# Queries and keys in a tile each, instead of two tiles of half the tokens each

## The chip, the cores and the metric

The kernel runs on one core of a Trainium2 chip. The metric is the device time of one execution in microseconds, as the median of several runs. Profiles are of one execution and show what each engine did: TensorE (PE, with its weight loads as PEld), VectorE (DVE), ScalarE (ACT), GpSimd (POOL), and SyncE (SP), which issues the transfers between the chip's main memory and its on-chip memory.

## The reference

A block of attention followed by a gated block, on 2048 tokens of width 640, in 32-bit floating point. What matters here is the attention: 32 heads of 20 columns, each token looking at itself and the 255 tokens before it.

```python
B, S, D = x.shape
H = 32; Dh = D // H; W = 256
qkv = (x @ wqkv).reshape(B, S, 3, H, Dh).transpose(2, 0, 3, 1, 4)
q, k, v = qkv[0], qkv[1], qkv[2]
scores = jnp.einsum("bhqd,bhkd->bhqk", q, k) * (Dh ** -0.5)
mask = (idx[:, None] - idx[None, :] >= 0) & (idx[:, None] - idx[None, :] < W)
scores = jnp.where(mask[None, None], scores, -1e9)
p = _softmax(scores, axis=-1)
o = jnp.einsum("bhqk,bhkd->bhqd", p, v)
return o.transpose(0, 2, 1, 3).reshape(B, S, D) @ wo
```

Around it: `h = x + A(layernorm(x))`, and then a gated block with a 2048 x 2048 product over the tokens, `h2 = h + B(layernorm(h))`.

## The kernel before

The program is written out in full, without loops on the chip, and the orders of the instructions of PE, DVE, ACT and SP are those of the source; those of POOL are set by a planner when the program is built. Waits between engines and transfers are put in by the framework, from what each instruction reads and writes.

**Stages.** Up to about 180 us the input is normalized and the value projection is made (`vgemm`); then the query and key projection (`qk_item`), whose last 16 items (`dense_tail`) lie beside the first maxima; from 243 to about 470 us the attention loop runs; after that come the output projection and the gated block.

**Queries and keys.** To keep the precision of 32 bits in 16-bit products, each query and key value is split into three bf16 parts (`split_qk`, L579 to L596), and the parts are written to `qk_d` in main memory (L595). From there four heads at a time, a *stack*, are loaded: 6 x 20 = 120 partitions hold six pairings of parts, so that one matmul over 120 rows gives the full product. There are 8 stacks and three places for them on the chip, used in turn: `slot0`, `slot1` and `xb` (the last is memory in which the input's normalized columns lay before). A place consists of two tiles of 16 KB a partition. Before the change, tile b of a place holds the tokens of half b (0 to 1023 or 1024 to 2047): first the queries of the four heads, then their keys. `qk_d` is laid out in the same way, by half, so one row of one part has the four heads' 1024 tokens next to each other.

`load_stack` (L298) issues 24 transfers on SP for each stack, 12 for half 0 and 12 for half 1, each of 20 rows and 160 KB. For the first use of a place it sets 32 rows of the keys to a constant with two clears on POOL (L304), one for each tile; the rows 120 to 122 of the keys that remain of it meet the rows 120 to 122 of the queries, which hold the negative row maxima in three parts, so that a product over 123 rows gives the score less the maximum. A stack is loaded during the 16 steps in which the stack two before it is scored: one transfer in even steps, two in odd ones.

**The loop** (L735 to L777) takes 128 steps, 16 for each stack; a step works on 128 tokens and four heads. In step s, for each head `hh`:

- `max_item` (L327) makes the products for the row maxima of the tokens 16 steps ahead: four strips of 32 queries, each against 288 keys (L341), side by side in the array's columns; DVE takes the maximum (L351). Where the 288 keys cross token 1024, the helper `tokens` (L314) gives two pieces, and each piece is a matmul with its own weight load. Stack 0's maxima are made before the loop, with one matmul of 128 queries and up to 384 keys (L345).
- `score_item` (L373) makes the scores: four strips of 32 keys, each against 288 queries (L394), again in two pieces where they cross token 1024; ACT takes the exponential (L397; in the last stack two heads at once, L399), and POOL clears what lies outside the window (L401, L404).
- `pv_item` (L407) multiplies the step before last with the values (L422); every second step a block of results is copied out (L438, L440) and stored (L441).

Every 8 steps `max_rows` (L354) turns the maxima, splits them into three parts, stores them to `m_d` (L366) and loads them into rows 120 to 122 of the queries of the half concerned (L368): the first half 8 steps before the stack is scored, the second as its scoring begins.

## Time and profile before

| | us |
|---|---|
| median of 3 runs (1126.02 to 1129.81) | 1126.63 |
| the profiled execution | 1125.76 |
| its span, first to last instruction | 1124.0 |
| from the loop's first exponential (242.94) to the last stack's first (448.77) | 205.83 |

The page of the profile gives each engine's busy time, the transfers and the chain of work that ended last. A table by stretch gives, for stretches of time, their length, then the busy time and number of instructions of each engine shown, the granted share of PE's clock, the share of the 16 transfer engines that was busy, and GB/s. In a timeline, the brackets at the end of a row give the idle time of that engine before the row and what ended it; "issue" says that the engine waited for nothing that the profile shows. In rows by source line, the three numbers after the colon are the least, median and greatest duration in nanoseconds. The names of tiles are shown without their numbers, so `slot` is either tile of slot0 or slot1, and `slot,slot` two of them.

### The profile page before, as it was taken

The numbers are of one execution on the slowest core, as the hardware profiler recorded it, in microseconds if no ns is written. First come the engines' busy times: TensorE is split into PE (matmuls) and PEld (weight loads), VectorE is DVE, ScalarE is ACT, GpSimd is POOL, SyncE is SP. The second block draws the span as 40 slices with busy tenths as digits, with TensorE's granted clock in tenths as the row PEclk, the third lists the DMA queues.
The fourth block names the chain that finished last, engine by engine and source line by source line (L and its number), as shares of the span: only waits on it lengthen the run. The fifth ranks groups of instructions, "written<-read, shape, count | busy, mean of one in ns | idle before, by whom it ended". The sixth has DMA issues, their size and how long they took to land.

```text
span 1124.0 us, 28713 instructions
## 1 busy us (share of the span) xinstructions
PE 1089.4 (97%) x11139; PEld 980.3 (87%) x11139; DVE 752.8 (67%) x2070; ACT 567.5 (50%) x1155; POOL 319.6 (28%) x447
## 2 busy tenths in 40 slices
PE   8999999989999999999999999999999999999998
PEld 8998887657877777699899999999999899999998
DVE  6643444779988999588877678655358974556542
ACT  4444443248988899735566567434347521222210
POOL 4324446766766666723200011000001000000000
PEclk9999999989999999999999999999999999999999
DMA  7834567545555555689554522242251563444321
GB/s 256 283 113 135 171 186 248 183 157 181 179 179 172 177 178 165 170 249 311 218 195 167 182 91 76 75 134 90 104 171 57 180 209 119 124 148 148 98 87 60
DMA packets 87672, 180.57 MB, mean 161 GB/s; under 512 B 11440, under 2 KB 45760, under 8 KB 83648
## 3 DMA queue, kind: packets, MB, share of 16 engines
q1 hardware_dynamic: 87536, 178.74, 49.8%
q8 instruction: 87, 1.43, 0.5%
q14 instruction: 49, 0.40, 0.1%
HBM read 120.82 MB, written 57.88 MB: 159 GB/s over the span
## 4 chain that ended last, share of the span: by engine, by line
PE 72%; DMA 8%; ACT 7%; DVE 6%; issue 3%; POOL 2%; SPq 1%; DVEq 0%; POOLq 0%; ACTq 0%
PE g L1136 22%; PE out_ps L1201 8%; ACT pt L397 5%; PE pv L422 4%; PE zb L1028 4%; PE qk L568 3%; PE qk L569 3%; PE qk L570 3%; PE bank L341 3%; PE bank L394 3%; PE zx L976 2%; PE zv L976 2%; PE zy L976 1%; PE wo_ps L101 1%; DMA o_d<-ot 1%
## 5 line engine op out<-in xcount | busy, mean ns | idle before, releaser
L397 ACT ACTIVATE pt<-bank 128x384 f32<-128x384 f32 (+1 forms) x452 | 180.1, 478 | 26.4 <-PE bank L394 16.2
L803 ACT ACTIVATE aw<-fx 128x512 fp32r<-128x512 f32 (+2 forms) x160 | 93.7, 596 | 173.5 <-PE g L1136 120.7
L1136 PE MATMUL g<-zl,aw 128*128 128x432 f32 x768 | 171.0, 358 | 0.0
L351 DVE CUSTOM_DVE_ANT_0 junk<-bank,strip 128x288 bf16<-128x288 f32 x392 | 156.7, 454 | 16.3 <-PE bank L341 13.8
L1136 PEld LDWEIGHTS g<-zl,aw 128*128 128x128 f32 x768 | 143.6, 188 | 5.9
L422 PE MATMUL pv<-pt,v_sb 128*32 128x192 f32 (+3 forms) x1984 | 129.6, 323 | 6.2 <-ACT ot L438 3.8
L1136 PE MATMUL g<-ze,aw 128*128 128x432 f32 x576 | 134.0, 360 | 0.3 <-DVE row L797 0.2
L797 DVE TENSOR_TENSOR aw<-fx,aw 128x512 fp32r<-128x512 f32 (+2 forms) x160 | 102.7, 647 | 37.1 <-ACT aw L803 35.8
L1136 PEld LDWEIGHTS g<-ze,aw 128*128 128x128 f32 x576 | 107.0, 188 | 6.7 <-ACT aw L803 1.2
L401 POOL TENSOR_SCALAR_AFFINE_SELECT pt<-pt 128x512 f32<-128x512 f32 x128 | 83.9, 656 | 62.7 <-ACT pt L397 60.2
L394 PE MATMUL bank<-slot 123*32 123x288 bf16 (+7 forms) x1296 | 94.4, 276 | 4.9 <-ACT pt L397 3.5
L1201 PE MATMUL out_ps<-wout,y_sp 128*128 128x320 f32 (+1 forms) x630 | 96.2, 309 | 0.4 <-ACT y_sp L140 0.4
L341 PE MATMUL bank<-slot 120*32 120x288 bf16 (+6 forms) x1280 | 92.2, 277 | 3.6 <-issue 1.6
L1028 PE MATMUL zb<-win,aw 128*128 128x432 f32 x480 | 95.4, 359 | 0.0
L1201 PEld LDWEIGHTS out_ps<-wout,y_sp 128*128 128x128 f32 (+1 forms) x630 | 94.1, 188 | 1.2 <-ACT y_sp L140 0.7
L87 POOL TENSOR_TENSOR mvz<-mvz,half 128x1 f32<-128x1 f32 x16 | 10.1, 633 | 298.8 <-DVE mvz L86 296.8
L1028 PEld LDWEIGHTS zb<-win,aw 128*128 128x128 f32 x480 | 89.9, 187 | 5.0 <-ACT row L803 0.3
L422 PEld LDWEIGHTS pv<-pt,v_sb 128*32 128x32 f32 x1984 | 59.9, 110 | 18.1 <-issue 9.9
L797 DVE TENSOR_TENSOR row<-g,row 128x432 f32<-128x432 f32 x80 | 48.2, 604 | 37.8 <-PE g L1136 36.9
L394 PEld LDWEIGHTS <-slot 123*32 123x32 bf16 x1728 | 58.5, 97 | 15.3 <-issue 6.0
L404 POOL TENSOR_SCALAR_AFFINE_SELECT pt<-pt 128x512 f32<-128x512 f32 x112 | 71.4, 637 | 0.0
L351 DVE CUSTOM_DVE_ANT_0 junk<-bank,mask 128x384 bf16<-128x384 f32 (+2 forms) x120 | 51.7, 447 | 21.1 <-PE bank L345 15.8
(196 smaller groups left out, 2247.1 us busy)
## 6 DMA issues: line engine op xcount, KB each, us to landing
slot<-qk_d SPq DMA_DIRECT2D x144, 160.0 KB
fx<-wsp_in SPq DMA_DIRECT2D x32, 512.0 KB
qk_d<-sg SPq DMA_DIRECT2D x40, 384.0 KB
fx<-hn_d SPq DMA_DIRECT2D x32, 320.0 KB
o_d<-ot SPq DMA_DIRECT2D x64, 128.0 KB
xb<-qk_d SPq DMA_DIRECT2D x48, 160.0 KB
z_d<-row SPq DMA_DIRECT2D x16, 432.0 KB
g_d<-row SPq DMA_DIRECT2D x16, 432.0 KB
```

The lines of the kernel that those rows point to most:

```text
L341: nc.tensor.matmul(ps[32 * j:32 * j + 32, o:o + w], one(st, 120, 0, hh, q0, 32), k, start=True, stop=True, tile_position=(0, 32 * j))
L351: nc.vector.tensor_tensor_reduce(out=junk[:, :n], in0=ps[:, :n], in1=keep, scale=1.0, scalar=NEG, op0=OP.add, op1=OP.max, accum_out=m_cols ...
L394: nc.tensor.matmul(ps[32 * i:32 * i + 32, b + o:b + o + w], one(st, 123, 1, hh, k0, 32), q, start=True, stop=True, tile_position=(0, 32 * i))
L397: nc.scalar.activation(pt[:, hh, :n], ps[:, :n], AF.Exp, scale=SCALE)
L401: nc.gpsimd.affine_select(out=pt[:, :, :P], in_=pt[:, :, :P], pattern=[[0, 4], [1, P]], base=0, channel_multiplier=-1, compare_op=OP.is_ge ...
L404: nc.gpsimd.affine_select(out=pt[:, :, 256:], in_=pt[:, :, 256:], pattern=[[0, 4], [-1, P]], base=-1, channel_multiplier=1, compare_op=OP. ...
L422: nc.tensor.matmul(ps[32 * hh:32 * hh + 32, a - 512 * c:b - 512 * c], v_sb[:, kb, v0:v0 + 32], pt[:, hh, a - kb * P:b - kb * P], start=fir ...
L797: (eng or nc.vector).tensor_tensor(out=out, in0=a, in1=b, op=op)
L803: nc.scalar.activation(out, a, AF.Copy)
L1028: nc.tensor.matmul(b[0][:, :HF], a[t][:, x, kk], win2[0][:, y, kk, h * HF:(h + 1) * HF], start=kk + x + y == 0, stop=kk == KD - 1 and x == 1)
L1136: nc.tensor.matmul(ps, w[m][:, x, k], zc[k][m][:, y], start=start and k + x + y == 0, stop=stop and k == 3 and x == 1, skip_group_check=True)
L1201: nc.tensor.matmul(ps[j][:, :HD], src[:w, a, k, :], e1["wout"][:w, b, k, j * HD:(j + 1) * HD], start=(k == 0 and a + b == 0), stop=(k == K ...
```

## The change

A place's two tiles now hold the queries (tile 0) and the keys (tile 1) of all 2048 tokens, in place of the two halves; `qk_d` loses its axis of halves, so that a row of one part and head has its 2048 tokens next to each other. `tokens` gives one access for any window, and `one` is gone: score and maximum matmuls that cross token 1024 are one matmul each. The loads keep their number and order (12 for the tokens below 1024, then 12 for the others), but each now takes, for each of its 20 rows, four separate runs of 1024 tokens. Both clears of a place go to the key tile, two heads each.

```diff
-    qk_d = dram.tile([2, 3, 2, 2 * DH, H // 2, S // 4], F32, name="qk_d")
+    qk_d = dram.tile([2, 3, 2 * DH, H // 2, S // 2], F32, name="qk_d")
...
-            slot_ap[i] = [h.bitcast(BF16).rearrange("p (a h t) -> p a h t", a=2, h=4) for h in halves]
-            slot_w[i] = [h.bitcast(F32).rearrange("p (a h t) -> p a h t", a=2, h=4) for h in halves]
+            slot_ap[i] = [h.bitcast(BF16).rearrange("p (h t) -> p h t", h=4) for h in halves]
+            slot_w[i] = [h.bitcast(F32).rearrange("p (h t) -> p h t", h=4) for h in halves]
...
-            st = slot_w[g % 3]
+            st, T = slot_w[g % 3], S // 4
             if g < 3:
-                for h in st:
-                    nc.gpsimd.memset(h[96:P, 1], ONES)
+                for i in range(2):
+                    nc.gpsimd.memset(st[1][96:P, 2 * i:2 * i + 2], ONES)
                     if g == 2:
                         yield
             for b in range(2):
                 for j, parts in enumerate(((0, 0), (0, 1), (0, 2), (1, 0), (1, 1), (2, 0))):
                     for a in range(2):
-                        src = qk_d[g // 4, parts[a], b, a * DH:(a + 1) * DH, g % 4 * 4:g % 4 * 4 + 4]
-                        nc.sync.dma_start(st[b][j:6 * DH:6, a], src)
+                        t = slice(b * T, (b + 1) * T)
+                        src = qk_d[g // 4, parts[a], a * DH:(a + 1) * DH, g % 4 * 4:g % 4 * 4 + 4, t]
+                        nc.sync.dma_start(st[a][j:6 * DH:6, :, t], src)
                         yield
 
         def tokens(st, rows, a, hh, t0, n):
-
-            o = 0
-            while o < n:
-                c, t = divmod(t0 + o, S // 2)
-                w = min(n - o, S // 2 - t)
-                yield o, w, st[c][:rows, a, hh, t:t + w]
-                o += w
-
-        def one(st, rows, a, hh, t0, n):
-            (_, _, x), = tokens(st, rows, a, hh, t0, n)
-            return x
+            return st[a][:rows, hh, t0:t0 + n]
...
-                    for o, w, k in tokens(st, 120, 1, hh, lo + skip * j, n):
-                        nc.tensor.matmul(ps[32 * j:32 * j + 32, o:o + w], one(st, 120, 0, hh, q0, 32), k,
-                                         start=True, stop=True, tile_position=(0, 32 * j))
+                    nc.tensor.matmul(ps[32 * j:32 * j + 32, :n], tokens(st, 120, 0, hh, q0, 32),
+                                     tokens(st, 120, 1, hh, lo + skip * j, n),
+                                     start=True, stop=True, tile_position=(0, 32 * j))
             else:
-                for o, w, k in tokens(st, 120, 1, hh, lo, n):
-                    nc.tensor.matmul(ps[:, o:o + w], one(st, 120, 0, hh, qb * P, P), k, start=True, stop=True)
+                nc.tensor.matmul(ps[:, :n], tokens(st, 120, 0, hh, qb * P, P), tokens(st, 120, 1, hh, lo, n),
+                                 start=True, stop=True)
...
-            nc.sync.dma_start(slot_w[g % 3][b][120:123, 0], rows.rearrange("a (h r) c -> a h (r c)", h=4))
+            t = slice(b * S // 4, (b + 1) * S // 4)
+            nc.sync.dma_start(slot_w[g % 3][0][120:123, :, t], rows.rearrange("a (h r) c -> a h (r c)", h=4))
...
-                for o, w, q in tokens(st, 123, 0, hh, kb * P + b, e - b):
-                    nc.tensor.matmul(ps[32 * i:32 * i + 32, b + o:b + o + w], one(st, 123, 1, hh, k0, 32), q,
-                                     start=True, stop=True, tile_position=(0, 32 * i))
+                nc.tensor.matmul(ps[32 * i:32 * i + 32, b:e], tokens(st, 123, 1, hh, k0, 32),
+                                 tokens(st, 123, 0, hh, kb * P + b, e - b),
+                                 start=True, stop=True, tile_position=(0, 32 * i))
...
-                T = S // 4
-                base = qk_d[m // 5, 0, c // 2, m % 5 * 8, 0, c % 2 * 256:c % 2 * 256 + 256]
+                T = S // 2
+                base = qk_d[m // 5, 0, m % 5 * 8, 0, c * 256:c * 256 + 256]
                 nc.sync.dma_start(bass.AP(tensor=base.tensor, offset=base.offset,
-                                          ap=[[T, P], [2 * 2 * DH * H // 2 * T, 3], [1, 256]]), sg.bitcast(F32))
+                                          ap=[[T, P], [2 * DH * H // 2 * T, 3], [1, 256]]), sg.bitcast(F32))
```

## The prediction

> **What bounds the kernel now.** First the profile's page: the span and the engines' sums.

> ```profile
> span 1124.0 us, 28713 instructions
> ...
> PE 1089.4 (97%) x11139; PEld 980.3 (87%) x11139; DVE 752.8 (67%) x2070; ACT 567.5 (50%) x1155; POOL 319.6 (28%) x447
> ```

> These are averages over stages; the change touches one, the attention loop from 243 to 449 us. So next comes the table by stretch for L397, the exponentials: each stretch is one stack of 16 steps with the same 64 of them (65 where an edge cuts one).

> ```profile
> 242.94:272.49 29.55, 25.66 (x64) 0.93 0.56 174
> 272.49:301.16 28.67, 25.64 (x64) 1.00 0.56 172
> 301.16:331.63 30.47, 25.33 (x64) 1.00 0.58 176
> 331.63:361.62 29.99, 25.51 (x65) 1.00 0.56 174
> 361.62:390.78 29.16, 25.36 (x64) 1.00 0.58 176
> 390.78:418.88 28.10, 25.43 (x64) 1.00 0.59 179
> 418.88:448.77 29.89, 25.46 (x65) 1.00 0.56 165
> ```

> The first numbers are the stretch and its length. ACT's exponentials fill 25.4 of 28.1 us in the fastest stack, and ACT has the ot copies beside them, so ACT sets the pace. Yet equal stacks differ by up to 2.4 us. Over 28.10 the others spend 1.45 + 0.57 + 2.37 + 1.89 + 1.06 + 1.79 = 9.1 us. The timeline shows where the largest parts lie.

> ```profile
> 317.11 0.31 PE L394 MATMUL bank<-xb 123*32 123x288 bf16 x4 [2.35 <-issue]
> ...
> 349.19 0.26 PE L341 MATMUL bank<-slot 120*32 120x224 bf16 x1 [1.62 <-issue]
> ...
> 380.17 0.30 PE L394 MATMUL bank<-slot 123*32 123x288 bf16 x3 [1.02 <-issue]
> ```

> PE stands still for 2.35, 1.62 and 1.02 us, together 4.99, and waits for nothing that the profile names ("issue"). It isn't caught up: the stack with 2.35 is the longest. Counting steps of 1.76 us (28.10 / 16) from the stack's start, the halts begin 7.7, 9.1 and 10.0 steps in: in or just behind steps 6 to 9, where windows cross token 1024 and PE has the most instructions. (The halt ends at a row's start and lasted its bracketed time; a row's start less that is 314.76, 347.57, 379.15.) I read them as a wait for PE's own program, from the page's DMA queues, the DMA view of two neighbouring stretches (309.6 to 314.1 us, and on to 315.6) and the table by stretch that ends at each halt.

> ```profile
> q8 instruction: 87, 1.43, 0.5%
> ```

> ```profile
> q1 hardware_dynamic: 280, 0.71, 60.2%
> ```

> ```profile
> q8 instruction: 1, 0.02, 5.8%
> ```

> ```profile
> 311.23:314.76 3.53, 3.53 (x140) 3.00 (x129) 3.53 (x19) 3.43 (x10) 2.62 (x5) 1.00 0.58 152
> 343.58:347.56 3.98, 3.93 (x138) 3.20 (x127) 3.86 (x19) 3.49 (x10) 2.90 (x6) 1.00 0.58 179
> 374.99:379.15 4.16, 4.08 (x138) 3.23 (x130) 3.92 (x19) 3.85 (x11) 3.24 (x7) 1.00 0.58 192
> ```

> **Fewer matmuls.** Rows by source line; a row with two tiles ("slot,slot") is the piece of a split item whose weights lie in the other half, one for each split.

> ```profile
> L394 PE MATMUL bank<-slot,slot x160: 177/224/270, 253.6 to 432.7; 123*32 123x128 bf16 x20, 123*32 123x96 bf16 x20, 123*32 123x32 bf16 x20, 123*32 123x64 bf16 x20
> L394 PE MATMUL bank<-xb,xb x64: 177/224/271, 311.3 to 403.7; 123*32 123x128 bf16 x8, 123*32 123x96 bf16 x8, 123*32 123x32 bf16 x8, 123*32 123x64 bf16 x8
> L394 PE MATMUL pair<-slot,slot x32: 177/224/270, 456.8 to 459.1; 123*32 123x128 bf16 x4, 123*32 123x96 bf16 x4, 123*32 123x64 bf16 x4, 123*32 123x32 bf16 x4
> L341 PE MATMUL bank<-slot,slot x160: 179/226/275, 256.7 to 436.3; 120*32 120x224 bf16 x20, 120*32 120x192 bf16 x20, 120*32 120x256 bf16 x20, 120*32 120x160 bf16 x20
> L341 PE MATMUL bank<-xb,xb x64: 176/228/275, 286.4 to 378.1; 120*32 120x256 bf16 x8, 120*32 120x224 bf16 x8, 120*32 120x192 bf16 x8, 120*32 120x160 bf16 x8
> L345 PE MATMUL bank<-slot,slot x8: 231/250/284, 211.6 to 218.0; 120*128 120x256 bf16 x4, 120*128 120x128 bf16 x4
> ```

> 256 + 224 + 8 = 488 matmuls go, with a weight load each: 976 of 22278 PE instructions, some 4 of 87 blocks. The columns streamed stay the same. Steps 6 and 7 of a stack (scores) and 8 and 9 (maxima) lose 16 pieces each. What a piece costs directly I read in the fastest stack, by four steps: 2 to 5, the split 6 to 9, 10 to 13.

> ```profile
> 394.09:401.26 7.17, 6.91 (x212) 5.88 (x208) 6.62 (x35) 6.83 (x18) 4.90 (x8) 1.00 0.61 175
> 401.26:408.68 7.42, 7.32 (x261) 6.38 (x257) 7.20 (x37) 6.84 (x17) 5.55 (x10) 1.00 0.62 196
> 408.68:415.76 7.08, 6.81 (x201) 6.13 (x196) 6.51 (x34) 6.74 (x17) 4.90 (x8) 1.00 0.49 154
> ```

> 7.42 against a mean of 7.13 is 0.29 us for 64 pieces, 4.6 ns each, so at most 7 x 0.29 = 2.0 us; at least nothing, as ACT is busy 6.8 us in each. I take **1.0**. The 8 in the dense stage and the 32 of the last stack lie beside ACT, POOL and other PE work: nothing.

> **The halts.** Split steps issue 518 records in 7.42 us, a block in 3.67; the others 817 in 14.25, a block in 4.47. A late block thus gains 0.8 us of cover: the three halts shrink by 0.8 each, 2.4 in all. The remaining 4.1 us of excess (9.1 - 4.99) are start-up in the first stack and waits under 1 us, some of them late blocks too; where the cover was the short one they vanish. I give them 1.8. Bounds: nothing if blocks come later by as much as PE slows, 8 if none comes late. I take **4.2**. What is late next is ACT, already the pace.

> [...]

> **The loads.** 24 loads a stack, in the same order on SP's queue; each changes from 20 runs of 8 KB to 80 of 2 KB, the same 160 KB, because a row's 1024-token half is no longer next to the next head's. The maximum's rows go from 3 runs to 12, and the stores at L595 keep their 384 of 1 KB at other strides. SP's issue times (least, median and most, in ns), by source line:

> ```profile
> L311 SPq DMA_DIRECT2D slot<-qk_d x144: 694/702/1885, 160.1 to 418.1; - x144
> L368 SPq DMA_DIRECT2D slot<-m_d x12: 265/272/380, 220.3 to 452.2; - x12
> L595 SPq DMA_DIRECT2D qk_d<-sg x40: 359/366/424, 92.9 to 242.9; - x40
> L160 SPq DMA_DIRECT2D m<-o_d x32: 302/434/1474, 457.7 to 527.2; - x32
> ```

> Upper end for the issue: by runs, (702 - 272) / 17 = 25 ns each, 80 give 2.2 us. Lower end: 160 runs take 434 ns at L160 and 384 take 366 at L595, so runs cost nothing. I take 0.75 us, near those rows. SP is then busy 24 x 0.75 + 8 x 0.37 (the o_d stores, priced as L595's) + 1.2 (the maximum's two stores and two loads) = 22 of 28.1 us a stack. Nobody waits for a load until the next stack's first maximum, nor for the maximum's rows until some 5 steps after their issue: **nothing**, while a load's issue stays under 1.0 us. The bytes are the same; should small runs move worse, q1's share of the engines, 60.2% in the stretch above, may grow by two thirds before they are full.

> **The constants.** Six clears of 32 rows on POOL keep their size, but both of a stack now go to the key tile. For the third that is the second half of xb, free only after the last projection item; before, one half was free early.

> ```profile
> L304 POOL MEMSET xb<- x2: 1800/1802/1804, 219.8 to 237.5; 32x2048 f32 x2
> ...
> 242.94 2.42 ACT L397 ACTIVATE pt<-bank 128x384 f32<-128x384 f32 x6 [4.17 <-POOL sg L592]
> ```

> One clear runs at 237.5, ahead of the POOL work for which the first exponential waits 4.17 us. If the other goes there too, the loop starts 1.8 us later. If it goes behind that work, only the third stack's key loads wait, and behind them on SP the first ot stores, for which there are six buffers. That work is ready while the first clear runs and stands earlier in the program, so I take **0**, bounds 0 and +1.8.

> **The sum.** 1.0 + 4.2 = 5.2 us. The profiled execution took 1125.76 (span 1124.0): 1120.6 by its own time. The median of the runs is 0.87 higher, 1126.63: **1121.4**.

> **Rivals.**
> (a) The blocks stay late: requests and transfers keep their distance and PE halts elsewhere. For: the last stretch, 29.89, has excess outside the crossing steps. Against: the three largest halts are all in them. Only the direct 1.0 is left: 1125.6. 0.20.

> [...]

> (b) The second clear delays the loop: 1121.4 + 1.8 = 1123.2. 0.06.
> (c) PE's issue sets the pace: each piece costs a matmul's turn, 7.17 us over 212, 34 ns, and 488 of them 16.6 us: 1110.0. The split steps' 4.6 ns a piece speak against it. With the upper ends of my own two terms, 2.0 and 8, it is 1116.6. Together 0.10.

> [...]

> (d) Slower: SP becomes the bound. At 1.4 us a load SP needs 24 x 1.4 + 4.2 = 37.8 us a stack against 28.1; six stacks are loaded in the loop, 58 us, 1184. It decides above 1.0 us a load. L595 speaks against it, the odd 702 of L311 for it. 0.07.
> (e) Slower: waits are set for whole tiles. Then score items wait for the second half's maximum rows in the query tile, which they don't read until step 6; the store alone takes 3.7 us to land, the load behind it some more, so about 5 us in each of seven stacks: 1156. Against it: ACT writes a part of aw while PE reads another. 0.05.

> ```profile
> 303.11 3.70 DMA m_d<-m
> ```

> ```profile
> 720.19 0.36 PE L1136 MATMUL g<-ze,aw 128*128 128x432 f32 x1
> 720.20 0.63 ACT L803 ACTIVATE aw<-fx 128x512 fp32r<-128x512 f32 x1 [3.85 <-PE g L1136]
> ```

> **Numbers.** The forecast has 0.52. About 0.3%, 3.4 us, is what a measurement of this kernel can tell from no change. Faster: forecast and (c), 0.62; within: (a) and (b), 0.26; slower: (d) and (e), 0.12. The range runs from (c)'s 1116.6 to 1127.5, (a) with the runs' scatter (1126.02 to 1129.81), and leaves out (d), (e) and (c)'s first price.

> **What would show it.** PE with 10651 matmuls and some 83 blocks on q8; no row with two tiles at L394 and L341; stacks of 28 to 28.5 us; no "issue" halt over 1 us in steps 6 to 9; L311 near 0.75 us; the first exponential's wait near 4.2 us. Wrong: halts of the old size at other steps (a), 6 us before the first exponential (b), L311 over 1 us (d), score items that wait for the slot's rows (e).

## The result: 7% slower, and the profile after

| | before | after |
|---|---|---|
| median of 6 runs each, us | 1129.42 (1126.02 to 1130.80) | 1210.16 (1207.22 to 1212.48) |
| ratio, with its 95% interval | 1 | 1.072 (1.070 to 1.075) |
| span of the profiled execution | 1124.0 | 1207.3 |
| first exponential of the loop | 242.94 | 254.56 |
| seven stacks, to the last stack's first exponential | 205.83 | 267.88 |
| from there to the end | 675.2 | 684.9 |

The forecast was 1121.4, so it missed by 89 us and by the sign. Of the 83.3 us between the two spans, 62.1 lie in the seven stacks of the loop, 11.6 ahead of it and 9.7 behind it. The first lines of the page, after:

```profile
span 1207.3 us, 27703 instructions
...
PE 1112.6 (92%) x10651; PEld 987.8 (82%) x10651; DVE 755.9 (63%) x2070; ACT 571.7 (47%) x1155; POOL 316.6 (26%) x447
```

PE has the 10651 matmuls that the prediction asked for, and q8 84 packets, and yet PE's share fell from 97% to 92%: it waits. Next comes the table by stretch, of the exponentials (L389 after), one stack of 16 steps a row.

```profile
254.56:291.29 36.73, 25.77 (x65) 0.92 0.50 153
291.29:331.08 39.79, 26.23 (x64) 0.89 0.43 131
331.08:371.52 40.44, 25.95 (x64) 0.84 0.43 129
...
450.66:488.75 38.09, 25.69 (x64) 0.95 0.44 133
488.75:522.44 33.69, 26.18 (x65) 0.87 0.42 121
sum 267.88, ACT 182.00; mean ACT 26.00
```

ACT has about the same work, 26 us, in stacks of 34 to 40 us, so it no longer sets the pace. The granted clock of PE, the number behind the count, fell to 0.84 to 0.95 where before it was 1.00 in six of seven stacks. The view of the waits, cut to PE, says for what it stands (us in total, times, longest):

```profile
PE bank L331 <- DMA slot<-qk_d: 15.3, 3, 5.5
PE bank L385 <- DMA slot<-m_d: 14.1, 5, 3.4
PE bank L331 <- DMA o_d<-ot: 11.4, 2, 6.1
PE bank L335 <- DMA slot<-qk_d: 7.1, 1, 7.1
PE bank L385 <- DMA xb<-m_d: 6.9, 2, 3.6
...
PE bank L331 <- DMA xb<-qk_d: 4.6, 1, 4.6
PE pair L385 <- DMA slot<-m_d: 4.3, 1, 4.3
```

These are 63.7 us at three points. The maximum items (L331) wait 31.3 us, six times: once at each boundary, where a new stack's maximum items begin. The score items (L385) wait 25.3 us, eight times: once a stack, for the maximum rows. And the first maximum item of all (L335), in the dense stage, waits 7.1. The name "o_d<-ot" in one of the rows is a wait for several transfers put down to the last of them; a maximum item reads nothing of it. In both of its waits the semaphore of the stack's last load makes its last update 0.1 to 0.4 us before PE goes on. The timeline of after at one boundary:

```profile
324.45 2.40 SPq L312 DMA_DIRECT2D slot<-qk_d  x3
...
330.42 0.30 PE L331 MATMUL bank<-slot,slot 120*32 120x128 bf16 x4 [5.22 <-DMA slot<-qk_d]
```

PE stands still from 325.20 and goes on when the last of the three loads has landed, issued at about 326.1. It is the 24th of the stack: keys of tokens 1024 to 2047. The item that waits reads keys and queries of tokens 0 to 127, whose loads were the stack's first 12. At the same boundary of the kernel before, the items went on at once:

```profile
298.62 2.20 SPq L311 DMA_DIRECT2D slot<-qk_d  x3
...
300.62 0.23 PE L341 MATMUL bank<-slot 120*32 120x128 bf16 x4
```

The last of those three loads was issued at about 300.1 too, half a microsecond ahead of the first item, and no bracket stands behind it: the half tile that it filled wasn't the one that the item read. The second point, in step 2 of the stack that begins at 331.08, in the timeline of after:

```profile
335.82 0.73 SPq L360 DMA_DIRECT2D xb<-m_d  x1
...
339.16 0.43 PE L385 MATMUL bank<-xb,xb 123*32 123x288 bf16 x4 [3.63 <-DMA xb<-m_d]
```

The load brings the maximum rows of tokens 1024 to 2047, the waiting score item reads queries 256 to 639. PE stood from 335.53, before that load was even issued. The loads of queries and keys themselves aren't slower: by the last update of each load's semaphore, a load in the loop lands a median of 3.7 us after its issue, against 4.0 before.

### The profile page after: what moved, and what is told of

It is laid out like the page before. It is cut to its first block, busy times and chain, and to the rows that moved or that the text cites. A ratio compares the mean times of both kernels' runs of the same rounds, so it can differ in the third digit from the quotient of the medians.

```text
span 1207.3 us, 27703 instructions
## 1 busy us (share of the span) xinstructions
PE 1112.6 (92%) x10651; PEld 987.8 (82%) x10651; DVE 755.9 (63%) x2070; ACT 571.7 (47%) x1155; POOL 316.6 (26%) x447
## 4 chain that ended last, share of the span: by engine, by line
PE 69%; DMA 10%; DVE 7%; ACT 6%; SPq 3%; issue 3%; POOL 2%; DVEq 0%; ACTq 0%; POOLq 0%
PE g L1128 20%; PE out_ps L1193 8%; PE pv L414 5%; PE qk L560 4%; PE qk L562 3%; PE qk L561 3%; PE bank L385 3%; PE bank L331 3%; ACT pt L389 3%; PE zb L1020 3%; PE zx L968 2%; PE zv L968 2%; DMA slot<-m_d 2%; DMA slot<-qk_d 1%; PE zy L968 1%
## 5 line engine op out<-in xcount | busy, mean ns | idle before, releaser
L389 ACT ACTIVATE pt<-bank 128x384 f32<-128x384 f32 (+1 forms) x452 | 183.7, 476 | 85.5 <-PE bank L385 45.4
L414 PE MATMUL pv<-pt,v_sb 128*32 128x192 f32 (+3 forms) x1984 | 134.6, 343 | 5.1 <-ACT ot L430 3.1
L331 PE MATMUL bank<-slot,slot 120*32 120x288 bf16 (+2 forms) x1280 | 97.2, 302 | 22.1 <-DMA slot<-qk_d 15.3
L385 PE MATMUL bank<-slot,slot 123*32 123x288 bf16 (+6 forms) x1296 | 99.5, 306 | 18.7 <-DMA slot<-m_d 14.1
L393 POOL TENSOR_SCALAR_AFFINE_SELECT pt<-pt 128x512 f32<-128x512 f32 x128 | 82.8, 647 | 99.2 <-ACT pt L389 90.9
L385 PEld LDWEIGHTS <-slot 123*32 123x32 bf16 x1536 | 51.7, 104 | 39.0 <-DMA slot<-m_d 16.0
L414 PEld LDWEIGHTS pv<-pt,v_sb 128*32 128x32 f32 x1984 | 62.6, 117 | 19.1 <-issue 10.3
L331 PEld LDWEIGHTS <-slot 120*32 120x32 bf16 x1280 | 45.6, 103 | 34.3 <-issue 14.7
```

The lines of the kernel that those rows point to most:

```text
L331: nc.tensor.matmul(ps[32 * j:32 * j + 32, :n], tokens(st, 120, 0, hh, q0, 32), tokens(st, 120, 1, hh, lo + skip * j, n), start=True, stop= ...
L385: nc.tensor.matmul(ps[32 * i:32 * i + 32, b:e], tokens(st, 123, 1, hh, k0, 32), tokens(st, 123, 0, hh, kb * P + b, e - b), start=True, sto ...
L389: nc.scalar.activation(pt[:, hh, :n], ps[:, :n], AF.Exp, scale=SCALE)
L393: nc.gpsimd.affine_select(out=pt[:, :, :P], in_=pt[:, :, :P], pattern=[[0, 4], [1, P]], base=0, channel_multiplier=-1, compare_op=OP.is_ge ...
L414: nc.tensor.matmul(ps[32 * hh:32 * hh + 32, a - 512 * c:b - 512 * c], v_sb[:, kb, v0:v0 + 32], pt[:, hh, a - kb * P:b - kb * P], start=fir ...
```

## The experiments

**Theory T1**: in the new tiles the two token halves of four heads lie interleaved, and a load of one half is taken to stand against reads of the other; so work waits for loads that it doesn't read. The rivals: a wait is set for the whole tile, whatever the region (R0); the loads as such have become too slow, by their issue on SP or by their 2 KB runs (R1); a merged matmul is itself slower (R2). The kernel of each diff is the one after the change, unless the text names another.

**1. The maximum rows by head.** One load of all four heads becomes four, each into one unbroken stretch.

```diff
-            nc.sync.dma_start(slot_w[g % 3][0][120:123, :, t], rows.rearrange("a (h r) c -> a h (r c)", h=4))
+            for h in range(4):
+                nc.sync.dma_start(slot_w[g % 3][0][120:123, h, t],
+                                  rows.rearrange("a (h r) c -> a h (r c)", h=4)[:, h])
```

> Edit: the load of the maximum rows of one token half into the query tile (line 360) is issued as four loads, one per head, in place of one load with four separate runs per row. Nothing else differs from the kernel after. Theory T1: waits come from regions that are taken to overlap because in the new tiles the two token halves of four heads lie interleaved; a load of one head's half touches one unbroken stretch and no longer stands against the reads of the other half. Then the halts of TensorE in step 2 of seven stacks (2.2 to 4.3 us each, 24 in sum with the ones after the loop, and slower clock behind them) go, and with the pieces around them a stack's step 2 falls from 6.1 to about 1.8 us: 7 x 4.3 = 30 us, about 1180 us. The halts at the stack boundaries (step 15) stay at 4.5 to 6 us. Rival R0 (a wait is set for the whole tile whatever the region): step 2 stays at 6 us, about 1210 us or a little more for three more loads a row half. Rival R1 (the load queue or its transfers are simply too slow for the new shapes): no gain, 1210 us or slower, since the queue gets more loads.

Measured: 1178.27 us in one run. PE's halts in step 2 are gone in all seven stacks: the steps take 1.75 to 1.85 us, where after they took 4.1 to 7.0. The seven stacks come to 241.13:

```profile
466.16:495.16 29.00, 25.61 (x64) 0.95 0.48 140
sum 241.13, ACT 179.89; mean ACT 25.70
```

The last stack, behind which no boundary follows, is down to 29.00. R0 falls: the same tile is written, only in stretches that don't span other heads. R1 falls for these rows, for SP issues more loads than before. Step 15 stays, at 7.8 us on the average of the six boundaries against 7.0 after.

**2. The loop's loads two a step.**

```diff
-            for _ in range(1 + s % 2 if s >= NT else 2 * min(s, 1)):
+            for _ in range(2 * min(s, 1)):
                 next(ld, None)
```

> Edit: the 24 loads of the next stack are issued two in every step from step 1 on in place of one and two by turns, so that the last one is issued by step 12 and not in step 14 or 15. Nothing else differs from the kernel after. T1: the first maximum item of a stack waits for the last second-half load of keys although it reads first-half tokens; with the last load landed some 4 us earlier the halts at six boundaries (4.5 to 6.1 us each, step 15 at 6.7 against 1.5 us) go: 6 x 5.2 = 31 us, about 1179 us. Step 2 stays at 6 us. Rival R1 (issue time of the loads, 0.76 us each, or their transfers bound the loop): a denser issue only moves the halt forward into steps 6 to 12, and the time stays within 8 us of 1210.

Measured: 1190.71 us in one run, 19 of the 31 us expected. At the boundary of the third stack PE still waits, but 0.51 us, the least of the six (4.66 at the first, 0.8 to 1.75 at the others); the halt in step 2 behind it grew to 5.01 (3.63 after):

```profile
326.68 0.24 PE L331 MATMUL bank<-slot,slot 120*32 120x128 bf16 x4 [0.51 <-DMA slot<-qk_d]
```

```profile
335.46 0.43 PE L385 MATMUL bank<-xb,xb 123*32 123x288 bf16 x4 [5.01 <-DMA xb<-m_d]
```

So the last load is what the boundary waited for, and a part of the gain is given back two steps later: PE comes there 5.1 us sooner than after (330.45 against 335.53), the load of the maximum rows is issued only 3.4 us sooner (332.45 against 335.82).

**3. The matmuls cut at token 1024 again**, in the new tiles, with `pieces` as before the change.

```diff
+                    for o, w in pieces(lo + skip * j, n):
+                        nc.tensor.matmul(ps[32 * j:32 * j + 32, o:o + w], tokens(st, 120, 0, hh, q0, 32),
+                                         tokens(st, 120, 1, hh, lo + skip * j + o, w),
+                                         start=True, stop=True, tile_position=(0, 32 * j))
...
```

> Edit: tiles, loads and stores are those of the kernel after, but every score and maximum matmul that spans token 1024 is cut there again into two, as before the change. T1 (the layout makes the loss, not the merged matmuls): about 1210 us or up to 6 us more, with halts of TensorE at steps 6 to 9 back in part. Rival R2 (a merged matmul is itself slower, by its operand's place or its wait): back to 1126 to 1135 us.

Measured: 1215.94 us in one run. R2 falls: the layout alone makes the whole loss, and merging takes some 6 us off it, by one run.

**4. Both edits, and the first stack's loads earlier in the dense stage.**

```diff
-                if n % 5 == 4:
-                    for _ in range(3):
+                if n in (4, 9):
+                    for _ in range(6):
                         next(ld0, None)
...
```

> Edit: the two edits before together (maximum rows by head, loads two a step), and the loads of the first stack in the dense stage issued earlier (six at the fifth and six at the tenth item of the tail in place of three at every fifth). T1: the losses add up, 30 at step 2, 31 at step 15 and 7.7 ahead of the first maximum item: 1210 - 69 = 1141 us, and down to 1130 if the clock, which is lower after each long halt, comes back with them. The two clears of the new key tile stay late (2 to 4 us). Rival R1 (issue or transfers): stays above 1180 us.

Measured: 1165.70 us, 25 more than expected. Step 2 is 1.7 to 1.85 us in all stacks but the first, but the boundaries kept 3.3 to 5.1 us each, and 5.6 stayed ahead of the first maximum item. R1 has a share here, as the timeline at one boundary shows:

```profile
313.18 3.16 SPq L312 DMA_DIRECT2D slot<-qk_d  x4
...
320.06 0.24 PE L331 MATMUL bank<-slot,slot 120*32 120x128 bf16 x4 [4.47 <-DMA o_d<-ot]
```

The last four loads of the stack, due by step 12, were issued at 313.18 to 316.3, in steps 14 and 15, as late as before the edit. SP is nearly full: 24 loads of 0.80 (0.75 and 0.05 to the next), 8 ot stores of 0.47, 8 maximum loads of 0.31 and 2 maximum stores of 0.45 are 26.3 us by this trace's typical entries, and waits for landings and for ot lie on top, in a stack that should take 28.

**5. The order of a stack's loads**: first halves of keys and queries, then second-half keys, second-half queries last.

```diff
-            for b in range(2):
+            for b, a in ((0, 1), (0, 0), (1, 1), (1, 0)):
                 for j, parts in enumerate(((0, 0), (0, 1), (0, 2), (1, 0), (1, 1), (2, 0))):
-                    for a in range(2):
...
```

> Edit: the same 24 loads of a stack at the same places of the program, in another order: first half of keys, first half of queries, second half of keys, second half of queries, in place of query and key row by turns (the second halves are the last 12 in both). So the second half of the keys is the 18th load and not the 24th; the last six are second-half queries. T1, sharpened: TensorE's streamed operand (keys in the maximum items) waits for both halves, its weight operand (queries) for its own half alone. Then the halts at six boundaries (5.2 us each) go although the last load lands as late as before, and with them the 7.7 us ahead of the first maximum item: 1210 - 31 - 8 = about 1171 us, up to 1185 if the step-2 halts grow as they did with the loads issued early. If the weights wait for both halves too, or if the queue as such is late (R1), 1205 to 1212 us.

Measured: 1185.39 us in one run. Step 15 is 1.50 us at every boundary, as before the change. The timeline at one of them:

```profile
320.31 2.40 SPq L311 DMA_DIRECT2D slot<-qk_d  x3
...
321.32 0.23 PE L330 MATMUL bank<-slot,slot 120*32 120x128 bf16 x4
```

Loads go out around the first maximum item as late as ever, and it doesn't wait: now they are second-half queries. So a maximum item's streamed operand, the keys, waits for both halves, and its weights, 32 queries, don't. The step-2 halts grew again (3.9 to 6.3 us of PE, the first stack's 2.2), and the dense halt stayed, at 7.5 us, which the expectation had wrong.

**6. That order and the maximum rows by head.**

> Edit: that order of loads together with the maximum rows loaded by head. T1: from the 1178 us of the maximum rows by head, the boundaries' 6 us each (step 15 at 7.5 against 1.5) and the 7.7 us ahead of the first maximum item go: 1178 - 36 - 8 = 1134 us. R1 (with the maximum rows by head the queue issues 24 loads, 8 short ones and 10 stores a stack, which took it up to the boundary when the loads were two a step): halts remain at step 15, 1150 us or more.

Measured: 1147.48 us in one run. Between the two figures expected: step 2 is clean from the second stack on, and step 15 is 2.9 to 6.3 us in five stacks. The halts of the second expectation are there, at a lower price than it gave: the late keys are back at the boundary. The 6 extra issues a stack are one likely cause; the stacks also became some 5 us shorter, and the two weren't told apart.

**7. The clears moved.** The keys of the third place go into the half of xb that is read out first.

```diff
-        add_slot(2, [h[:, :2 * S] for h in xb])
+        add_slot(2, [h[:, :2 * S] for h in xb[::-1]])
```

> Edit: the same, and in the third place the keys lie in the tile that is read out sooner, so that its two clears no longer stand late on GpSimd's queue ahead of the split of the last dense product. T1: the wait of ScalarE for that split (5.6 us after the change, 4.2 before) falls by 2 to 3 us: 1131 us; with all four losses gone the remainder is the prediction's own sum, 1121 to 1126 us, if the later stages too give back what they lost. Same as e9 within 1 us if the clears were hidden.

Measured: 1145.36 us (1144.40 to 1148.66), 14 more than expected, for step 15 still takes 2.4 to 7.0 us in five stacks. The loop starts at 253.08 in place of 254.6 in the kernel of 6. What the clears did is plain in the timeline of after:

```profile
246.12 1.80 POOL L304 MEMSET xb<- 32x2048 f32 x1 [0.38 <-PE qk L562]
248.00 1.16 POOL L584 TENSOR_TENSOR sg<-rest,sg 128x512 bf16<-128x512 f32 x1
...
249.22 1.80 POOL L304 MEMSET xb<- 32x2048 f32 x1
...
253.39 1.14 POOL L584 TENSOR_TENSOR sg<-rest,sg 128x512 bf16<-128x512 f32 x1
254.56 1.64 ACT L389 ACTIVATE pt<-bank 128x384 f32<-128x384 f32 x4 [5.62 <-POOL sg L584]
```

Both stand ahead of the split for which the first exponential waits, 5.62 us against 4.17 before.

**8. The kernel of 7 with the matmuls cut again.**

> Edit: the same kernel as the one with the clears moved, but score and maximum matmuls are cut at token 1024 again: 976 matmul and weight-load instructions more, nothing else. It measures by itself what merging them is worth. The prediction's terms (1.0 direct, 4.2 of TensorE's waits for its own program) give this kernel 5.2 us more than its partner; a price of 34 ns an instruction slot gives 16 us more; nothing if the pieces were hidden.

Measured: 1149.64 us (1146.80 to 1152.77), 4.3 more than its partner.

**9. Whole-row loads** in the kernel of 7: 12 of 320 KB a stack from the third on, one a step.

```diff
+            for t, a in [(slice(b * T, (b + 1) * T), a) for b in range(2) for a in (1, 0)] if g < 2 else [
+                    (slice(0, 2 * T), a) for a in (1, 0)]:
...
-            for _ in range(1 + s % 2 if s >= NT else 2 * min(s, 1)):
+            for _ in range(min(s, 1)):
```

> Edit: the kernel with maximum rows by head and moved clears, and from the third stack on a stack is loaded with 12 loads of whole rows (2048 tokens, 320 KB), one a step, in place of 24 of half rows; the first two stacks keep half rows, first halves of keys and queries, then second halves. It tests what was left at the boundaries (step 15 at 2.4 to 7.0 us in five stacks, some 13 us over 1.5 in sum): if it is the queue's own time (some 27 us of issuing a stack of 29 us, so that the loads fall behind), half as many issues let step 15 fall to 1.5 us: 1145 - 14 = about 1131 us. If it is the waits' reach over both halves, a load over both halves makes it no better: 1145 us or more. If a load of twice the bytes takes twice as long to issue, 1145 us too.

Measured: 1148.87 us (1144.08 to 1153.06): no gain on 1145.36, where 1131 was expected. A load of twice the bytes issues in a median of 0.722 us (the 24 into xb), against 0.749 in the kernel of 7 (the 48 into xb), but the first boundary took 8.47 us, the others 1.5 to 3.4:

```profile
278.52 0.72 SPq L311 DMA_DIRECT2D xb<-qk_d  x1
...
287.12 0.30 PE L330 MATMUL bank<-xb,xb 120*32 120x128 bf16 x4 [6.67 <-issue]
```

The profile names nothing that ended this wait, but the last update of that load's semaphore in the trace is at 286.81. Here the item does read what the last load brings: whole rows of queries. From its issue to the item are 8.6 us, against 4.3 at the boundary of after shown above (about 326.1 to 330.42). The last four loads, issued from 275.07 to 278.52, land 1.6 to 2.0 us apart, as if each stood behind the one before; why wasn't settled.

**10. That kernel with the matmuls cut again.**

> Edit: the same with the score and maximum matmuls cut at token 1024 again (976 instructions more, nothing else). It measures what merging is worth without the halts at the boundaries in the way: 5.2 us more than its partner by the prediction's two terms (1.0 direct, 4.2 of TensorE's waits for its own program blocks, to be seen as halts of steps 6 to 10); 16 us by a price for each instruction; 0 to 1 us if the halts moved elsewhere.

Measured: 1154.90 us (1150.42 to 1157.17), 6.0 more than its partner.

**11. Strips in the dense stage** in the kernel of 9, for the first eight blocks of the first stack.

```diff
-                    max_item(u // NT, u % NT, hh, False)
+                    max_item(u // NT, u % NT, hh, u < 8)
```

> Edit: the whole-row kernel, and the first stack's maximum items of the first eight blocks, which lie in the dense stage, are computed in four strips of 32 queries, as in the loop, in place of one matmul with 128 queries as weights. In the loop the 32-column weights waited for their own half alone; if it is the same here, the first maximum item waits for 18 of 24 loads in place of all, and the 7.8 us halt ahead of it falls to about 2 us: 5 to 6 us less than its partner, about 1125 us. If the 128-column weights were not what waited for the second half, the halt stays at 7.8 us and the time at its partner's.

Measured: 1146.43 us (1143.21 to 1152.57), where 1125 was expected. The wait behaves as expected: 1.92 us against the partner's 7.77, and the first item at 186.09, where the partner's stood at 192.45.

```profile
186.09 0.24 PE L330 MATMUL bank<-slot,slot 120*32 120x128 bf16 x4 [1.92 <-DMA slot<-qk_d]
```

But the loop starts at 253.63 against 252.26: with 32 items in strips the way from the first item to the loop takes 67.5 us in place of 59.8. The 6.4 us are spent again in the same stage. So 128-column weights did wait for the second half, and 32-column ones don't.

**12. Keys whole, queries in halves.** The kernel of 7, from the third stack on with 6 whole-row loads of keys and then 12 of queries, in the kernel after's pace; strips for two blocks in the dense stage.

```diff
+            for t, a in (((first, 1), (first, 0), (second, 1), (second, 0)) if g < 2 else
+                         ((whole, 1), (first, 0), (second, 0))):
...
```

> Edit: maximum rows by head and moved clears as before; from the third stack on the keys are loaded first, in 6 whole-row loads, then the queries in 12 half-row loads, in the kernel after's pace (18 loads in place of 24); in the dense stage the first two blocks' maximum items (8 of 64) are computed in strips of 32 queries. If the streamed keys are all that the first maximum item of a stack waits for in both halves, the 12th load is the last that it needs, some 7 steps ahead of it: step 15 falls to 1.5 us at every boundary, the loop to about 200 us (205.8 before, less the 5 that merging is worth). The first maximum item starts at 186 to 187 us in place of 192, and with 8 items in strips in place of 32 the loop starts 4 to 6 us earlier than the 252 to 254 us of the other mended kernels. In sum 1148.9 - 13 - 5 = about 1130 us, the level of the kernel before. If the boundary residue has another cause, 1140 us or more.

Measured: 1130.98 us (1127.55 to 1135.89), ratio to before 1.003 (1.001 to 1.005). Step 15 is 1.50 us at every boundary. The stacks, by the exponentials:

```profile
305.65:334.06 28.41, 25.55 (x64) 1.00 0.57 180
...
sum 203.75, ACT 178.75; mean ACT 25.54
```

The loop is 2.1 us shorter than before the change, the granted clock is 1.00 from the second stack on, and the first maximum item starts at 185.09.

**13. The kernel of 12 without strips, with four more dense steps ahead of the first maximum item.**

> Edit: the same loads; in the dense stage no strips, but the first maximum item is placed four dense steps later (24 steps ahead of it in place of 20). The halt ahead of it falls by the 2.8 us or so that these steps take, and the last maximum items stand without dense work between them. Loop as with the keys loaded whole; start of the loop 250 to 253 us, 2 us or more later than its partner if the strips keep what they gain; the sum 1130 to 1134 us.

Measured: 1130.43 us (1127.13 to 1135.56), the same as its partner. The loop starts at 249.44, just ahead of the 250 to 253 expected, and takes 199.3 us.

**14. The kernel of 12 with the matmuls cut again**: what merging is worth where no load is late.

> Edit: the kernel with the keys loaded whole and two blocks in strips, with the score and maximum matmuls cut at token 1024 again, nothing else. What merging is worth where no load is late at a boundary: its partner stood at 1131.0 us, so 1136.2 us by the prediction's two terms (1.0 direct, 4.2 of waits for program blocks, halts of steps 6 to 10 of the loop), 1147 us by 34 ns an instruction slot, 1131 to 1132 us if the gain in the loop had come from the loads.

Measured: 1140.21 us (1136.86 to 1143.59), 9.2 more than its partner, where 5.2 were expected; ratios to before 1.011 (1.008 to 1.014) and 1.003 (1.001 to 1.005). The table by stretch over the same four steps, 6 to 9, of seven stacks, the cut kernel first, then its partner:

```profile
257.41:268.22 10.81, 6.82 (x16) 1.00 0.66 239
...
408.04:419.34 11.30, 7.11 (x16) 0.85 0.62 212
...
sum 63.05, ACT 47.54; mean ACT 6.79
```

```profile
257.36:264.48 7.12, 6.63 (x16) 1.00 0.69 244
...
sum 51.59, ACT 46.52; mean ACT 6.65
```

And the halts of the cut kernel, from its timeline, three of them:

```profile
266.99 0.20 PE L337 MATMUL bank<-slot,slot 120*32 120x64 bf16 x2 [2.52 <-issue]
...
381.24 0.24 PE L394 MATMUL bank<-slot,slot 123*32 123x192 bf16 x3 [2.14 <-issue]
...
415.08 0.32 PE L337 MATMUL bank<-slot,slot 120*32 120x96 bf16 x2 [2.06 <-issue]
```

The four steps differ by 11.5 us, the whole loops by 8.8 (212.59 against 203.75). The partner has no halt for "issue" over 0.7 us in its loop. That these halts are waits for PE's program shows on q8, the queue that carries it (87 packets for 22278 instructions of PE and PEld before, 84 for 21302 after): ahead of the first of them no block came from 259.3 to 264.4 us, then one between 264.4 and 265.5:

```profile
q8 instruction: 1, 0.02, 5.5%
```

In the trace, a block of q8 starts 2.5 to 2.6 us ahead of the restart in all three.

**15 and 16. The second stack's keys whole too**, in the kernel of 12, with 24 and with 20 dense steps ahead of the first maximum item.

> Edit: the same kernel with merged matmuls, the second stack's keys loaded whole too (18 loads in the dense stage in place of 24), and 24 dense steps ahead of the first maximum item. If the queue's time in the dense stage holds up the dense stores and so the loop's start, the loop starts at 243 to 244 us and the kernel comes to 1127 to 1129 us, as before within what can be told; if not, 1130 to 1131 us.

> Edit: the same without the four dense steps (20 ahead of the first maximum item). If the queue's time in the dense stage counts, 1128 to 1130 us against 1131.0 of the kernel with 24 loads of the second stack; if not, 1131 us. Against its partner with 24 steps it tells whether the halt of 1.2 us ahead of the first maximum item is worth having.

Measured: 1125.60 us (1123.78 to 1129.22) with 24, ratio to before 0.9986 (0.9969 to 1.0003); 1128.31 (1123.70 to 1132.82) with 20, ratio 1.0003 (0.9984 to 1.0021). The first is the best of all kernels, 1.9 us ahead of before by the medians, which can't be told from no change. Its loop starts at 243.63 us, as expected, and takes 200.05, 5.8 less than before. Late blocks of the program aren't quite gone even here: in step 8 of the third stack PE stands for 1.52 us, and a block of q8 starts 2.6 us ahead of the restart here too.

```profile
317.40 0.30 PE L332 MATMUL bank<-slot,slot 120*32 120x288 bf16 x3 [1.52 <-issue]
```

## Why the prediction was wrong

**The step that failed** is the sentence in the part on the loads that nobody waits for a load until the next stack's first maximum, nor for the maximum's rows until 5 steps after their issue, and with it the 0.05 for rival (e). It priced the loads' issue and bytes, and took for granted that work waits only for what it reads. In the new tiles it doesn't: 64 us of waits by the trace of after, and slower work behind them. The runs give the parts: the maximum rows by head take 32 us off (1210.16 to 1178.27), the keys' second half ahead of the late queries another 31 (to 1147.48), the clears 2 (to 1145.36), fewer loads of keys and an earlier first item in the dense stage 14 (to 1130.98). Single runs stand behind 1178.27 and 1147.48, so the first three parts are good to some 4 us only.

**Rival (e) had half of it.** It named the score items, step 2, the maximum rows of the second half and some 5 us in each of seven stacks, and the trace shows that place. Its rule, whole tiles, was wrong: rows loaded by head end the wait in the same tile. And it missed the larger half, the boundaries and the dense stage, where the same holds for the loads of keys. The evidence against it was from another kind of access: that ACT writes a part of aw while PE reads another shows nothing on a load whose four runs enclose the tokens that PE reads. The contrast was in the change itself: before, a load filled one half tile; after, its target spans the whole row of four heads.

**Step by step:**
- *Fewer matmuls, 1.0, and the halts, 4.2*: right in kind and near in sum, but the direct part too large and the halts too small. In the kernel after itself, steps 6 to 9 of the seven stacks take 50.05 us where they took 57.95; the table by stretch before, with its sum, and after:

```profile
401.26:408.68 7.42, 6.72 (x16) 1.00 0.62 196
...
sum 57.95, ACT 46.71; mean ACT 6.67
```

```profile
267.53:274.64 7.11, 6.64 (x16) 1.00 0.59 181
...
sum 50.05, ACT 46.54; mean ACT 6.65
```

  The prediction read the group of 7.42 us as one without a halt, but its step 8 takes 2.24 us where undisturbed stacks take 2.03. Undisturbed groups of cut matmuls take 7.20 or 7.21 (experiment 14), of merged ones 7.12: 0.09 us a stack and 0.6 in seven, in place of 1.0. The rest of the 7.9 us between the two sums is halts. Merging doesn't have all of them to its credit: with the matmuls cut in the new tiles (experiment 3) these steps take 50.82 us, and step 10 takes 3.4 us more in seven stacks than after, 4.2 in all. A likely reason, not tested, is that PE's long waits for loads give the blocks of its program time to arrive. In time, merging measured 4.3, 6.0 and 9.2 us in three pairs of kernels, against the 5.2 of the sum. Rival (a), of which only the direct 1.0 would be left, falls, though halts of up to 1.52 us remain in steps 6 to 9 of merged kernels; (c)'s 16.6 us of issue falls too. (c)'s second price, both terms at their upper ends and 10 us together, is near the largest of the three.
- *The loads' issue, 0.75 us*: right, 0.763 at L312, and the issue of the maximum's rows rose from 0.272 to 0.728, 0.9 us a stack that the sum of 22 us didn't have. But the point at which SP becomes the bound, 1.0 us a load, was too high: it left out 0.05 us behind each entry and the waits that stand in the queue. Experiments 4 and 6 met it at 0.75 us a load. In the kernel after itself (d) isn't what happened: experiment 5 moved no load earlier and its boundaries don't wait.
- *The clears, 0*: wrong, by about rival (b)'s price. Both went ahead of the split that the first exponential waits for; moving them gave 1.5 us of loop start and some 2 us of time, against a single run.

**Left open.** The clock: the stacks with long halts show 0.84 to 0.95, and their step 0 takes 2.83 us against 1.83 where no halt precedes it, so a part of the 62 us is slower work behind the halts; what grants it wasn't tried. The runs show which loads were waited for, not the rule by which a read is taken to overlap a load: streamed operands and 128-column weights waited for the other half, 32-column weights didn't. And behind the loop the profiled executions of the changed kernels take 678 to 689 us against 675.2; 4.3 us of that are a score item's wait in the kernel after, for the rest little is edited there, and the timed runs scatter by as much.

## What to carry to other kernels

When halves of a buffer that arrive at different times are interleaved in one tile (63.7 us of PE's waits here), ask of each reader not only what it reads but which loads' targets enclose it, and put those loads first, in unbroken stretches, or out of the way. A saving in an engine's instructions can be real and still be lost ten times over to a wait that the layout brings, so price the layout on its own. A queue can be full before the sum of its entries fills the stage, as SP's was in experiment 4 with 26.3 us of entries in a stack that should take 28: add the gap behind each entry and the waits that stand in it.

## What the runs showed of the hardware

- PE's waits for its own program are worth more than their count suggests. With the matmuls cut, the four steps of seven stacks took 57.95 us before and 63.05 in experiment 14; with 976 instructions fewer they took 50.05 and 51.59, though the page shows 84 packets on q8 in place of 87 or 88. In the trace of before, a packet of q8 starts 2.4 to 3.0 us ahead of each of the three restarts that the prediction lists, and the next one 1.4 to 1.6 us behind it.
- The issue of a load follows neither bytes nor runs alone. These are the maximum's rows, in 12 runs and by head in 3 (after, then experiment 7), least, median and most in ns; the 160 KB loads went only from 702 to 763 for 80 runs in place of 20, and the whole-row loads of 320 KB into xb took 694/722/1220.

```profile
L360 SPq DMA_DIRECT2D slot<-m_d x12: 707/728/742, 230.4 to 526.3; - x12
```

```profile
L360 SPq DMA_DIRECT2D slot<-m_d x48: 252/263/357, 232.8 to 470.4; - x48
```
